# Attention and MLP on one core: five other token blocks, weights rounded through DRAM, and k halves stacked by transfers

## The chip, the cores and the metric

The kernel runs on one core of one Trainium2 chip, as one program. The metric is device time in microseconds (us). Of the kernel before there are three timed runs: 794.15, 796.12 and 800.07 us, median 796.12. A core has five engines that work side by side, each through its own list of instructions in order: PE (TensorE, matmuls; its weight loads are shown apart as PEld), DVE (VectorE), ACT (ScalarE), POOL (GpSimd) and SP (SyncE, which here issues every transfer). They wait for one another by semaphores.

## The reference, cut to what matters

```python
q, k, v: (4, 8, 576, 64)                       # batch, heads, tokens, head size
q_rot, k_rot = rotate(q), rotate(k)            # x1*cos - x2*sin, x1*sin + x2*cos
scores = q_rot @ k_rot.T / sqrt(64)
attn = softmax(scores)                         # max taken off, exp, divided by the sum
x = attn @ v, heads side by side               # (4, 576, 512): 2304 tokens of 512
xn = (x - mean(x)) / sqrt(var(x) + 1e-6) * g_ln
out = x + relu(xn @ w_ch1) @ w_ch2             # w_ch1: 512 x 2048, w_ch2: 2048 x 512
```

Everything is float32. A large matmul is made of three rounded ones (`fp32r`): an operand is split into a rounded part ("high") and the rest ("low"), and high by high, low by high and high by low are added up.

## The kernel before, in words

**Attention** goes through 16 pairs of heads, four for each of the four batches; two heads of 64 fill the 128 partitions. For pair `i`, `prepare` loads q and k with their swapped halves, rotates them (L315 to L319), rounds them (L322, L324), takes the low part (L327, L329) and lays high and low parts one above the other in the "stacks" that the score matmuls read (L423). For q, and for the k of pairs 4 to 15, SP does the stacking by transfers from SBUF to SBUF (L378 to L391). For the k of pairs 1 to 3 PE does it: two small matmuls with a doubled identity for each half and part (L357, 24 in all), each followed by a copy out of PSUM by ACT or DVE (L180). A pair then has nine score units: scores on PE (L423; the ninth L428 and L431), their maximum on DVE (L454), the exponential on ACT (L466). The results `p` are transposed on PE (L510, L524, L551) into PSUM tiles `t`, of which there are two, copied out by ACT or DVE (L180), and multiplied with `v` (L592, L596) in two parts, 256 and 320 queries, again into a `t` tile. DVE scales that by the inverse sums into the output tile `xt` (L607).

**The MLP** runs over blocks of tokens. `BLOCKS` has five: one of 256 tokens and four of 512. When all pairs of a block's tokens are in `xt`, `layer_norm` centres, scales and rounds it, with sums over the 512 features made by PE (L643, L677, L689). Then the block passes over the weights: 32 units of 12 matmuls (L814), each unit one 512x128 piece of a weight matrix in high and low parts; the moving side is the block, so a matmul has as many columns as the block has tokens. Units of the first matrix end in relu on ACT (L830) and the low part on DVE (L834); those of the second are added to `xt` (L844), and after the last four the block is stored (L853) and its `xt` tile is free. There is one `xt` buffer of 256 tokens and three of 512.

**The weights** come in as float64 (`w64`, 512 KB for a unit). `decode` makes float32 of them with two ACT operations (L742, L745), two on DVE (L748, L754) and one on POOL (L751), writes the result to DRAM (`keep`, L757) and at once splits it (`split`: high part by ACT, L774; low part by POOL or DVE, L778) for the first pass. The four later passes load the float32 piece from DRAM (`load_w`, L787) and split it again. A float32 piece sits in a ring of three buffers `f`, its high and low parts in a ring of three buffers `w`; in the first pass an `f` buffer is free only when both the write to DRAM and the split are done.

**The order of the work** is fixed when the program is built. Every step is a task with a duration for each engine that may do it, a priority and the ring buffers that it takes and gives. `Plan.run` walks through the tasks in planned time, starts whatever can start in order of priority, and so writes one list of instructions for each engine; attention's tasks have the priority of a nominal time (`nominal`, set by `FIRST`, `FAST`, `PACE`), the decode tasks one set by `DECODE0` and `DECODE1`, and the MLP matmuls the last of all, so that they fill what attention leaves. What a task really takes does not change the order: an engine that is at an instruction whose operand isn't there waits, with all that is behind it.

Of the kernel before, what the change touches and what calls it, by code (L numbers as in the profile page):

```python
# [10 lines left out]
F32 = mybir.dt.float32  # L11
# [23 lines left out]

BLOCKS = [(0, 256)] + [(t, BLOCK) for t in range(256, N_TOK, BLOCK)]
PARTS = slice(0, 2 * P), slice(2 * P, S)
# [101 lines left out]
def rope_attention_then_ln_mlp(  # L139
# [24 lines left out]

    cp, xp, qkp, vpool, xtp = pool("const"), pool("x", RINGS["x"]), pool("qk", RINGS["stk"]), pool("v", RINGS["v"]), pool("xt")
    pp, ptp, smp, lnp = pool("p", RINGS["p"]), pool("pt"), pool("small", 4), pool("ln")
# [6 lines left out]
    def raw(t):  # L173
        return t.bitcast(F32)
# [55 lines left out]
    def first_pair():  # L230
# [12 lines left out]
        def dma(kb, o, i, after=(), prio=-90.0):  # L243
            return add({"SP": kb / 230}, lambda: SP.dma_start(o, i), after, prio)

# [47 lines left out]
    def prepare(i):  # L293
# [5 lines left out]
        for n, nm in ((1, "k"), (0, "q")):  # L299
# [12 lines left out]
            def op(step, nm=nm):  # L312
                a, b = st["x", i, nm]
                if step == 0:
                    eng().tensor_tensor(out=a, in0=a, in1=rope_sb[:, 0], op=ALU.mult)  # L315
                elif step == 1:
                    eng().tensor_tensor(out=b, in0=b, in1=rope_sb[:, 1], op=ALU.mult)
                elif step == 2:
                    eng().tensor_tensor(out=a, in0=a, in1=b, op=ALU.add)  # L319
                elif step == 3 and nm == "k" and i < NPB:  # L320
                    h = st["hik", i] = lnp.tile([P, NC, BLOCK], F32R, name="xh").rearrange("p a s -> p (a s)")[:, :S]
                    ACT.copy(h, a)  # L322
                elif step == 3:
                    ACT.copy(b.bitcast(F32R), a)  # L324
                elif nm == "k":
                    kl = st["kl", i] = qkp.tile([P, S], F32R, name="k_lo")
                    eng().tensor_tensor(out=kl, in0=a, in1=raw(st["hik", i]) if i < NPB else b, op=ALU.subtract)  # L327
# [5 lines left out]
            ld = add({"SP": 576 / 230}, load, [ev.get("l_qs")] + free0, p - 8, take=ring, name=f"load{i}{nm}")  # L333
            r0 = add(how2, lambda op=op: op(0), [ld], p, name=f"r0.{i}{nm}")
# [12 lines left out]
            stacks = []  # L347
            if nm == "k" and i < NPB:

                done[nm, 0], done[nm, 1] = [], []  # L350
                for j in range(2):
                    for low in range(2):
                        for a in range(2):
                            def put(j=j, low=low, a=a):
                                ps = st["st", i, j, low, a] = mp.tile([P, 512], F32, name="m")
                                x = st["kl" if low else "hik", i]
                                PE.matmul(ps[:, :HS], lhsT=twice[j], rhs=x[:, KEYS[a]], start=True, stop=True)  # L357

                            def out(j=j, low=low, a=a):
                                t = ("skl", "sk")[1 - low]  # L360
                                if (t, i) not in st:
                                    st[t, i] = qkp.tile([P, 2, S], F32R, name=("stack_k", "stack_kl")[low])
                                copy(st[t, i][:, j, KEYS[a]], st.pop(("st", i, j, low, a))[:, :HS])

                            end = j == 1 and a == 1 and low == 1
                            m_ = add({"PE": 0.14}, put, [lo if low else hi, ev["c3"]], p + 0.6 + j, take=["m"], give=["x" + nm] if end and ring else [], lag=0.2, name=f"st{i}{j}{low}{a}")
                            o_ = add({"ACT": 0.40, "DVE": 0.44}, out, [m_], p + 0.6 + j, give=["m"], behind=done[nm, 1][:1])
                            done[nm, j].append(o_)
                            if j == 0:
                                done[nm, 1].append(o_)  # L370
                continue
            for j in range(2):
# [20 lines left out]
                kb = 288 if nm == "k" else 144  # L393
                stacks.append(add({"SP": kb / 200}, stack_hi, [hi], p + 0.6 + j, name=f"sh{i}{nm}{j}"))
                last = add({"SP": kb / 200}, stack_lo, [lo], p + 0.7 + j, behind=list(stacks), name=f"sl{i}{nm}{j}", give=ring if j else [])
                stacks.append(last)
# [3 lines left out]
    def load_v(i):  # L400
# [3 lines left out]

        ev["v", i] = add({"SP": 320 / 230}, load, [ev["l_qs"]], nominal(i, 0) - 4, take=["v"], name=f"v{i}")

# [26 lines left out]
    def attention(i):  # L433
# [45 lines left out]
        def sums(a):  # L479
# [5 lines left out]
            units = range(4) if a == 0 else range(4, 9)  # L485
            return add({"DVE": 0.36}, f, [exps[n] for n in units], nominal(i, units[-1]) + 0.5)

# [84 lines left out]
        for a in range(2):  # L572
# [25 lines left out]
            def scale(a=a):  # L598
                s = PARTS[a]
                ps = st.pop(("pv", i, a))  # L600
                for n, lo, hi in pieces(b, a):
                    if ("xt", n) not in st:
                        w = BLOCKS[n][1]
                        st["xt", n] = xtp.tile([P, NC, w], F32, name=f"xt{w}", bufs=RINGS[f"xt{w}"])
                    x = slice(lo - b * S - s.start, hi - b * S - s.start)
# [15 lines left out]
    def layer_norm(n):  # L621
        t0, W = BLOCKS[n]
        Q = W // 4
        parts = [(b, a) for b in range(B) for a in range(2) if any(m == n for m, _, _ in pieces(b, a))]
        done = [ev["x", NPB * b + c, a] for b, a in parts for c in range(NC)]
        b1, a1 = parts[-1]
        N = nominal(NPB * b1 + NPB - 1, 8 if a1 else 4) + 6
        z = {}
        two = {"POOL": 1.4 * W / 512, "DVE": 0.9 * W / 512}
        f = W / 512  # L630
# [5 lines left out]

        prev = done
# [63 lines left out]
        for c in range(NC):  # L701
# [12 lines left out]

            s = add({"DVE": 0.9 * f}, scale, [t], N + 0.1 * c)
            h = add({"ACT": 0.6 * f}, high, [s] + ([ready[0]] if c else []), N + 0.1 * c, take=["xn"] if c == 0 else [], name=f"xn{n}")
# [6 lines left out]
    def decode(k):  # L723
# [34 lines left out]

        t0 = add({"SP": 512 / 230}, load, [ev["l_qs"]] if k == 0 else [], prio - 8, behind=[ev["w64", k - 1]] if k else [], take=["w64"], name=f"w64.{k}")
        ev["w64", k] = t0  # L760
        t1 = add({"ACT": 0.67}, a1, [t0], prio, behind=[ev["a1", k - 1]] if k else [], take=["f"])
        ev["a1", k] = t1
        t2 = add({"ACT": 0.67}, a2, [t1], prio)
        t3 = add({"DVE": 0.56}, d1, [t1], prio)
        t4 = add({"POOL": 1.4}, p1, [t2, t3], prio)
        t5 = add({"DVE": 1.0}, d2, [t4], prio, give=["w64"])
        ev["ws", k] = add({"SP": 256 / 230}, keep, [t5], prio + 6)
        split(k, t5, prio)
        add({"NONE": 0.0}, lambda: None, [ev["ws", k]] + ev["wr", k], prio, give=["f"])

    def split(k, there, prio):
# [8 lines left out]
        ev["w", k] = add({"ACT": 0.62}, hi, [there], prio, behind=[ev["w", k - 1]] if k else [], take=["w"], name=f"w{k}")  # L780
        how = {"POOL": 1.35, "DVE": 0.9} if k < len(UNITS) else {"POOL": 1.35}
        ev["wr", k] = [add(how, lo, [ev["w", k]], prio, give=["f"] if k >= len(UNITS) else [])]

    def load_w(k, prio):
# [3 lines left out]

        ev["f", k] = add({"SP": 256 / 230}, load, [ev["ws", k % len(UNITS)]], prio, behind=[ev["f", k - 1] if k > len(UNITS) else ev["w", k - 1]], take=["f"], name=f"f{k}")
        split(k, ev["f", k], prio)  # L790


    def mlp_unit(k, prev):
# [45 lines left out]
        else:  # L839
# [7 lines left out]
            if u >= NF + 3 * NC:  # L847
# [7 lines left out]

                add({"SP": 256 / 230}, store, [r], 1e5, give=[f"xt{W}"] if c == NC - 1 else [], name=f"store{n}.{c}")

# [32 lines left out]

DEBUG = 1

# [51 lines left out]
```

## Time and profile before

| | us |
|---|---|
| median of three runs | 796.12 |
| the profiled execution, its own time | 797.25 |
| its span, first to last instruction | 795.5 |
| PE busy | 711.6 |
| DVE, POOL, ACT busy | 453.3, 444.8, 407.2 |
| mean granted TensorE clock | 0.972 |

A matmul counts as busy from its start to the modelled end of its drain, and matmuls that follow each other overlap; so how fast PE works through a row of them is read from their starts, not from their mean duration. In the line `L814 PE MATMUL m<-hh,w 128*128 128x512 f32 x512` the name `m` is a PSUM tile, `w` the weights, `hh` the moving side. Columns of a table of windows are: the stretch, its length, busy us and number of instructions of PE, PEld, DVE, ACT and POOL, the granted clock, the busy share of the DMA engines, and what they moved.

### The profile page before, as it was taken

Reading aid. Unit: us, or ns where it says so; the run is one execution under the profiler, and the core shown is the slowest. Engines: PE = TensorE matmul, PEld = TensorE weight load, DVE = VectorE, ACT = ScalarE, POOL = GpSimd, SP = SyncE. Lnnn points to the kernel's source line nnn. Section 1 sums busy time; section 2 is a strip of 40 time slices with the busy share of each in tenths; the row PEclk is TensorE's granted clock in tenths of the full one; section 3 lists DMA queues with packets and bytes.
Section 4 is the critical chain, followed back from the end, with each engine's and each line's share of the span. In section 5 each row is a group of like instructions: output and inputs, shape, how many; then the busy total and the mean of one; then the engine's idle time right before and its main releaser. Section 6 shows DMA issues by size and latency. Waiting matters only on the chain. (4 is left out here: it accounts for less than half of the span.)

```text
span 795.5 us, 11683 instructions
## 1 busy us (share of the span) xinstructions
PE 711.6 (89%) x3986; PEld 558.3 (70%) x3986; DVE 453.3 (57%) x756; ACT 407.2 (51%) x890; POOL 444.8 (56%) x326
## 2 busy tenths in 40 slices
PE   2788887998797877789989999999999999999998
PEld 1666555786575665668768888776787788878886
DVE  7768767778788897754783234644526522322222
ACT  3667657767575667545653344554424333433231
POOL 2587366777749665666874453114447444454442
PEclk9989999999899998899999999999999999999999
DMA  7655866668875676866636334112234232353332
GB/s 216 205 160 160 267 160 167 170 208 243 238 218 143 196 232 200 214 181 194 155 114 185 98 101 126 54 54 69 79 94 133 85 101 93 93 149 103 92 95 78
DMA packets 65691, 117.83 MB, mean 148 GB/s; under 512 B 11472, under 2 KB 23520, under 8 KB 65632
## 3 DMA queue, kind: packets, MB, share of 16 engines
q1 hardware_dynamic: 65632, 117.09, 51.1%
q8 instruction: 31, 0.51, 0.3%
q14 instruction: 28, 0.23, 0.1%
HBM read 79.76 MB, written 13.18 MB: 117 GB/s over the span
## 5 line engine op out<-in xcount | busy, mean ns | idle before, releaser
L778 POOL TENSOR_TENSOR w<-f,w 128x512 fp32r<-128x512 f32 x145 | 190.8, 1318 | 230.1 <-ACT w L774 213.0
L814 PE MATMUL m<-hh,w 128*128 128x512 f32 (+1 forms) x640 | 197.7, 380 | 6.0 <-DVE w L778 3.2
L774 ACT CAST w<-f 128x512 fp32r<-128x512 f32 x160 | 99.0, 620 | 200.2 <-PE m L814 101.1
L814 PE MATMUL m<-xh,w 128*128 128x512 f32 (+1 forms) x640 | 195.2, 375 | 1.9 <-ACT std L681 1.1
L814 PEld LDWEIGHTS m<-hh,w 128*128 128x128 f32 x640 | 119.4, 192 | 29.8 <-DVE w L778 4.0
L814 PEld LDWEIGHTS m<-xh,w 128*128 128x128 f32 x640 | 118.4, 189 | 24.3 <-ACT std L681 1.4
L454 DVE TENSOR_REDUCE mx<-sc 128x1 f32<-128x576 f32 x144 | 105.7, 748 | 38.7 <-PE sc L423 31.6
L466 ACT ACTIVATE p<-sc,mx 128x576 f32<-128x576 f32 x144 | 106.0, 739 | 35.0 <-DVE mx L454 22.9
L814 PE MATMUL m<-hl,w 128*128 128x512 f32 (+1 forms) x320 | 119.3, 373 | 1.8 <-DVE hl L834 1.8
L814 PE MATMUL m<-xl,w 128*128 128x512 f32 (+1 forms) x320 | 118.3, 370 | 0.0
L834 DVE SCALAR_TENSOR_TENSOR hl<-m,hh 128x512 fp32r<-128x512 f32 (+1 forms) x80 | 50.8, 635 | 110.4 <-ACT hh L830 110.2
L510 PE MATMUL t<-ident,p 128*128 128x128 f32 x512 | 84.4, 292 | 28.1 <-DVE xt L607 7.1
L844 DVE TENSOR_TENSOR xt<-xt,m 128x512 f32<-128x512 f32 (+1 forms) x80 | 50.5, 631 | 94.7 <-PE m L814 94.6
L510 PEld LDWEIGHTS t<-ident,p 128*128 128x128 f32 x512 | 61.5, 147 | 47.0 <-issue 9.3
L180 ACT COPY pt<-t 128x512 f32<-128x512 f32 (+1 forms) x86 | 47.1, 550 | 65.4 <-PE t L510 56.4
L423 PE MATMUL sc<-stack_k,stack_q 128*128 128x288 f32 x252 | 64.6, 339 | 8.2 <-ACT p L466 7.9
L596 PE MATMUL t<-pt,v 128*64 128x320 f32 (+1 forms) x512 | 71.6, 424 | 0.0
L814 PEld LDWEIGHTS m<-hl,w 128*128 128x128 f32 x320 | 61.5, 192 | 13.0 <-DVE hl L834 2.6
L180 DVE COPY pt<-t 128x512 f32<-128x512 f32 (+1 forms) x74 | 46.0, 621 | 37.6 <-PE t L510 31.4
L814 PEld LDWEIGHTS m<-xl,w 128*128 128x128 f32 x320 | 60.7, 190 | 9.2
L751 POOL TENSOR_TENSOR f<-f,w 128x512 int32<-128x512 int32 x32 | 42.9, 1339 | 37.6 <-ACT w L745 19.3
L596 PEld LDWEIGHTS t<-pt,v 128*64 128x64 f32 x512 | 35.1, 141 | 33.3 <-issue 15.1
(128 smaller groups left out, 972.5 us busy)
## 6 DMA issues: line engine op xcount, KB each, us to landing
f<-w SPq DMA_DIRECT2D x128, 256.0 KB
w<-in_w1p SPq DMA_DIRECT2D x16, 512.0 KB
w<-f SPq DMA_DIRECT2D x32, 256.0 KB
w<-in_w2p SPq DMA_DIRECT2D x16, 512.0 KB
xk<-in_qk SPq DMA_DIRECT2D x14, 576.0 KB
xq<-in_qk SPq DMA_DIRECT2D x14, 576.0 KB
stack_q<-xq SPq DMA_DIRECT2D x56, 144.0 KB
stack_kl<-k_lo SPq DMA_DIRECT2D x52, 144.0 KB
```

What stands on the lines that cost most here:

```text
L180: (ACT.copy if plan.engine == "ACT" else DVE.tensor_copy)(o, i)
L423: PE.matmul(ps[:, a, :HS], lhsT=sq[:, j, q], rhs=y[:, j, KEYS[a]], start=y is sk, stop=y is skl)
L454: DVE.tensor_reduce(out=mx, in_=st["ps", i, n][:, :, :HS], axis=AX.XY, op=ALU.max, negate=True)
L466: ACT.activation(out=halves(p), in_=st.pop(("ps", i, n))[:, :, :HS], func=AF.Exp, bias=st.pop(("mx", i, n)), scale=1.0, accum_out=total)
L510: PE.transpose(ps[:, k], p[:, j, j * T + k * P : j * T + (k + 1) * P], ident)
L596: PE.matmul(ps[r], lhsT=v[:, k, r], rhs=pt[:, j, k], start=False, stop=k == 3)
L751: POOL.tensor_tensor(out=z["f"], in0=z["f"], in1=z["c"], op=ALU.add)
L774: ACT.copy(w[:, 0].rearrange("p a n -> p (a n)"), st["f", k].bitcast(F32))
L778: eng().tensor_tensor(out=w[:, 1], in0=st.pop(("f", k)).bitcast(F32), in1=raw(w[:, 0]), op=ALU.subtract)
L814: PE.matmul(ps, lhsT=wt, rhs=x, start=c + m == 0, stop=c + m == NC + 1)
L834: DVE.scalar_tensor_tensor(out=h2, in0=z["ps"][:, :W], scalar=0.0, in1=raw(h1), op0=ALU.max, op1=ALU.subtract)
L844: DVE.tensor_tensor(out=o, in0=o, in1=z["ps"][:, :W], op=ALU.add)
```

## The change

The diff does five things.

- `BLOCKS` becomes 512, 512, 512, 384 and 384 tokens. All `xt` tiles now have room for 512 tokens, in one ring of three.
- A decoded weight piece goes into a buffer of its own (`d`, ring of two) and from there to DRAM, and nothing else; it is not split from there. All five passes, the first too, load from DRAM. `f` keeps three buffers, `w` gets four. `load_w` gets a priority ahead of attention's (-2.0).
- k of pairs 1 to 3 is stacked by SP transfers as that of the others (`KPE` is 0).
- Layer norm may start its sums feature block by feature block, and its priority is 10 us earlier.
- The ring `p` has three buffers instead of four. The planner's durations and its transfer rate have other values, and decode has other priorities.

```diff
-BLOCKS = [(0, 256)] + [(t, BLOCK) for t in range(256, N_TOK, BLOCK)]
+BLOCKS = [(0, 512), (512, 512), (1024, 512), (1536, 384), (1920, 384)]
...
-RINGS = {"sc": 2, "t": 2, "m": 2, "p": 4, "p9": 1, "pt0": 1, "pt1": 1, "x": 1, "stk": 2, "v": 2, "inv": 2, "w64": 2, "f": 3, "w": 3, "h": 4, "xn": 1, "ln": 1, "xt256": 1, "xt512": 3}
+RINGS = {"sc": 2, "t": 2, "m": 2, "p": 3, "p9": 1, "pt0": 1, "pt1": 1, "x": 1, "stk": 2, "v": 2, "inv": 2, "w64": 2, "f": 3, "d": 2, "w": 4, "h": 4, "xn": 1, "ln": 1, "xt": 3}
-DECODE0, DECODE1 = 30.0, 4.5
+DECODE0, DECODE1 = 70.0, 4.0
+RATE = 300.0
+KPE = 0
+EARLY = 10.0
...
-                elif step == 3 and nm == "k" and i < NPB:
+                elif step == 3 and nm == "k" and i < KPE:
...
-            if nm == "k" and i < NPB:
+            if nm == "k" and i < KPE:
...
-            ev["x", i, a] = add({"DVE": 0.5}, scale, [t, rd], N, behind=lead, take=[f"xt{BLOCKS[n][1]}" for n in fresh], give=["t"] + (["inv"] if a else []))
+            ev["x", i, a] = add({"DVE": 0.5}, scale, [t, rd], N, behind=lead, take=["xt"] * len(fresh), give=["t"] + (["inv"] if a else []))
...
-        done = [ev["x", NPB * b + c, a] for b, a in parts for c in range(NC)]
+        done = [[ev["x", NPB * b + c, a] for b, a in parts] for c in range(NC)]
...
+        N = min(N - EARLY, 1e5)
+        prev = done[0]
         for c in range(1, NC):
-            prev = [add(two, lambda c=c: acc(c), prev, N, take=["ln"] if c == 1 else [], name=f"ln{n}")]
+            prev = [add(two, lambda c=c: acc(c), prev + done[c], N, take=["ln"] if c == 1 else [], name=f"ln{n}")]
...
-            f = z["f"] = st["f", k] = wp.tile([P, NC * P], I32, name="f", bufs=RINGS["f"])
+            f = z["f"] = wp.tile([P, NC * P], I32, name="d", bufs=RINGS["d"])
...
-        t5 = add({"DVE": 1.0}, d2, [t4], prio, give=["w64"])
-        ev["ws", k] = add({"SP": 256 / 230}, keep, [t5], prio + 6)
-        split(k, t5, prio)
-        add({"NONE": 0.0}, lambda: None, [ev["ws", k]] + ev["wr", k], prio, give=["f"])
+        t5 = add({"DVE": 1.25}, d2, [t4], prio, give=["w64"])
+        ev["ws", k] = add({"SP": 256 / RATE}, keep, [t5], prio, give=["d"])
...
-        how = {"POOL": 1.35, "DVE": 0.9} if k < len(UNITS) else {"POOL": 1.35}
-        ev["wr", k] = [add(how, lo, [ev["w", k]], prio, give=["f"] if k >= len(UNITS) else [])]
+        how = {"POOL": 1.35, "DVE": 1.0} if k < 2 * len(UNITS) else {"POOL": 1.35}
+        ev["wr", k] = [add(how, lo, [ev["w", k]], prio, give=["f"])]
...
     for k in range(len(UNITS) * NB):
-        if k >= len(UNITS):
-            load_w(k, 9e5 + k)
+        load_w(k, -2.0)
         mlp_unit(k, None)
```

Three places show what this does to the lists. The numbers behind the names are buffer numbers; line numbers of the changed kernel are two or three higher than before.

The first is PE's list around the first `pt`-by-`v` product of pair 6 (tiles `pt0`), in the midst of attention. Before:

```order
L592 MATMUL t_2315<-p40_2169,v_1765 128x256
L596 MATMUL t_2315<-pt0_2168,v_1765 64x256 x8
L423 MATMUL sc_2332<-stack_k_1842,stack_q_2016 128x288 x2
L423 MATMUL sc_2332<-stack_kl_1876,stack_q_2016 128x288 x2
L510 MATMUL t_2339<-ident_165,p_2070 128x128 x4
L423 MATMUL sc_2348<-stack_k_1842,stack_q_2016 128x288 x2
L423 MATMUL sc_2348<-stack_kl_1876,stack_q_2016 128x288 x2
L814 MATMUL m_2303<-xh_1607,w_2283 128x256
L814 MATMUL m_2303<-xl_1608,w_2283 128x256
L814 MATMUL m_2303<-xh_1607,w_2283 128x256 x2
```

And now:

```order
L595 MATMUL t_2096<-p40_1983,v_1692 128x256
L599 MATMUL t_2096<-pt0_1982,v_1692 64x256 x8
L513 MATMUL t_2113<-ident_165,p_2010 128x128 x4
L426 MATMUL sc_2122<-stack_k_1469,stack_q_1499 128x288 x2
L426 MATMUL sc_2122<-stack_kl_1520,stack_q_1499 128x288 x2
L431 MATMUL sc_2131<-k_lo_1485,diag0_170 128x288 x2
L434 MATMUL sc_2131<-stack_k_1469,last_q0_172 128x288 x4
L513 MATMUL t_2143<-ident_165,p_2010 128x128 x4
L815 MATMUL m_2076<-xh_1775,w_1067 128x512
L815 MATMUL m_2076<-xl_1776,w_1067 128x512
L815 MATMUL m_2076<-xh_1775,w_1067 128x512 x2
```

The MLP matmuls of the first pass stand among attention's as before, but each has 512 columns instead of 256. Counted over the whole list, 918 MLP matmuls stand ahead of attention's last one before (384 of 256 columns, 534 of 512) and 1002 behind it; now 924 stand ahead, all of 512 columns, and 996 behind it (228 of 512 columns, 768 of 384). The first MLP matmul stands in pair 5 before and in pair 6 now.

The second is SP's list from the write of pair 7's first sums on. Before:

```order
L574 DMA sums7_0_113<-row0_2669 4x128
L378 DMA stack_q_2671<-xq_2519 64x576
L735 DMA w64_2692<-in_w1p 128x1024
L757 DMA w8_147<-f_2635 128x512
L385 DMA stack_q_2671<-xq_2519 64x576 x2
L310 DMA xk_2765<-in_qk 128x1152
L584 DMA inv_2784<-sums7_0_113 64x2x128 x2
```

And now:

```order
L577 DMA sums7_0_113<-row0_2464 4x128
L788 DMA f_2498<-w23_146 128x512
L587 DMA inv_2531<-sums7_0_113 64x2x128 x2
L760 DMA w10_149<-d_2446 128x512
L738 DMA w64_2539<-in_w2p 128x1024
L760 DMA w11_150<-d_2515 128x512
L738 DMA w64_2591<-in_w2p 128x1024
L788 DMA f_2594<-w8_147 128x512
L381 DMA stack_k_2607<-xk_2312 64x576
```

Loads of `f` (L788) now stand between attention's transfers; each may go only when a split has freed an `f` buffer. Ahead of the write of pair 12's first sums there are 11 such loads before and 48 now. The transfers that stand from pair 6's first write of sums to that of pair 10 hold 28.6 MB before and 37.9 MB now, and the loads of the k stacks of pairs 1 to 3 are 24 more transfers of 144 KB near the list's start.

The third is DVE's list now, where the first pass ends; `xt_592` is the tile of the first 512 tokens, `xt_3851` that of tokens 1536 to 1919, in the same buffer ring:

```order
L845 TENSOR_TENSOR xt_592<-xt_592,m_3773 128x512
L845 TENSOR_TENSOR xt_592<-xt_592,m_3788 128x512
L779 TENSOR_TENSOR w_3835<-f_3753,w_3835 128x512
L835 SCALAR_TENSOR_TENSOR hl_3838<-m_3808,hh_3837 128x512
L609 TENSOR_TENSOR xt_1726<-t_3234,inv_3017 128x128
L609 TENSOR_TENSOR xt_3851<-t_3234,inv_3017 128x192
L609 TENSOR_TENSOR xt_1726<-t_3737,inv_3421 128x128
L609 TENSOR_TENSOR xt_3851<-t_3737,inv_3421 128x192
```

Pair 8's second part (`t_3234`) is the first to write `xt_3851`, and waits until the first block has gone through its whole pass and is stored; its PSUM tile `t` is held till then, and pair 9's (`t_3737`) with it. Before, with one more `xt` buffer, no such wait stood in pairs 8 to 11; one for the last block stood, and stands, in pair 12. Of the 160 low parts of weights DVE makes 15 before and 34 now, POOL the others.

More of the change, by code (lines that the diff above doesn't have):

```diff
@@ L243, in dma @@
         def dma(kb, o, i, after=(), prio=-90.0):
-            return add({"SP": kb / 230}, lambda: SP.dma_start(o, i), after, prio)
+            return add({"SP": kb / RATE}, lambda: SP.dma_start(o, i), after, prio)
         def tt(o, a, b, op, after, dur=0.76, prio=-80.0, e="DVE"):
@@ L326, in op @@
                     kl = st["kl", i] = qkp.tile([P, S], F32R, name="k_lo")
-                    eng().tensor_tensor(out=kl, in0=a, in1=raw(st["hik", i]) if i < NPB else b, op=ALU.subtract)
+                    eng().tensor_tensor(out=kl, in0=a, in1=raw(st["hik", i]) if i < KPE else b, op=ALU.subtract)
                 else:
@@ L332, in prepare @@
             free0 = ev["stk", 0][1] + ev["diag", 0] + [ev["s", 0, 1]] if i == 2 else []
-            ld = add({"SP": 576 / 230}, load, [ev.get("l_qs")] + free0, p - 8, take=ring, name=f"load{i}{nm}")
+            ld = add({"SP": 576 / RATE}, load, [ev.get("l_qs")] + free0, p - 8, take=ring, name=f"load{i}{nm}")
             r0 = add(how2, lambda op=op: op(0), [ld], p, name=f"r0.{i}{nm}")
@@ L393, in prepare @@
                 kb = 288 if nm == "k" else 144
-                stacks.append(add({"SP": kb / 200}, stack_hi, [hi], p + 0.6 + j, name=f"sh{i}{nm}{j}"))
-                last = add({"SP": kb / 200}, stack_lo, [lo], p + 0.7 + j, behind=list(stacks), name=f"sl{i}{nm}{j}", give=ring if j else [])
+                stacks.append(add({"SP": kb / RATE}, stack_hi, [hi], p + 0.6 + j, name=f"sh{i}{nm}{j}"))
+                last = add({"SP": kb / RATE}, stack_lo, [lo], p + 0.7 + j, behind=list(stacks), name=f"sl{i}{nm}{j}", give=ring if j else [])
                 stacks.append(last)
@@ L403, in load @@
             SP.dma_start(v, vp[divmod(i, NPB)])
-        ev["v", i] = add({"SP": 320 / 230}, load, [ev["l_qs"]], nominal(i, 0) - 4, take=["v"], name=f"v{i}")
+        ev["v", i] = add({"SP": 320 / RATE}, load, [ev["l_qs"]], nominal(i, 0) - 4, take=["v"], name=f"v{i}")
     def pieces(b, a):
@@ L485, in sums @@
             units = range(4) if a == 0 else range(4, 9)
-            return add({"DVE": 0.36}, f, [exps[n] for n in units], nominal(i, units[-1]) + 0.5)
+            return add({"DVE": 0.6}, f, [exps[n] for n in units], nominal(i, units[-1]) + 0.5)
         inverse = [sums(0), sums(1)]
@@ L602, in scale @@
                     if ("xt", n) not in st:
-                        w = BLOCKS[n][1]
-                        st["xt", n] = xtp.tile([P, NC, w], F32, name=f"xt{w}", bufs=RINGS[f"xt{w}"])
+                        st["xt", n] = xtp.tile([P, NC, BLOCK], F32, name="xt")
                     x = slice(lo - b * S - s.start, hi - b * S - s.start)
@@ L628, in layer_norm @@
         z = {}
-        two = {"POOL": 1.4 * W / 512, "DVE": 0.9 * W / 512}
+        two = {"POOL": 1.5 * W / 512, "DVE": 1.05 * W / 512}
         f = W / 512
@@ L713, in low @@
                 eng().tensor_tensor(out=st["xl", n][:, c], in0=z["xc"][:, c], in1=raw(st["xh", n][:, c]), op=ALU.subtract)
-            s = add({"DVE": 0.9 * f}, scale, [t], N + 0.1 * c)
+            s = add({"DVE": 1.1 * f}, scale, [t], N + 0.1 * c)
             h = add({"ACT": 0.6 * f}, high, [s] + ([ready[0]] if c else []), N + 0.1 * c, take=["xn"] if c == 0 else [], name=f"xn{n}")
@@ L757, in keep @@
             SP.dma_start(scratch[u], z["f"].bitcast(F32))
-        t0 = add({"SP": 512 / 230}, load, [ev["l_qs"]] if k == 0 else [], prio - 8, behind=[ev["w64", k - 1]] if k else [], take=["w64"], name=f"w64.{k}")
+        t0 = add({"SP": 512 / RATE}, load, [ev["l_qs"]] if k == 0 else [], prio - 8, behind=[ev["w64", k - 1]] if k else [], take=["w64"], name=f"w64.{k}")
         ev["w64", k] = t0
-        t1 = add({"ACT": 0.67}, a1, [t0], prio, behind=[ev["a1", k - 1]] if k else [], take=["f"])
+        t1 = add({"ACT": 0.67}, a1, [t0], prio, behind=[ev["a1", k - 1]] if k else [], take=["d"])
         ev["a1", k] = t1
         t2 = add({"ACT": 0.67}, a2, [t1], prio)
-        t3 = add({"DVE": 0.56}, d1, [t1], prio)
+        t3 = add({"DVE": 0.7}, d1, [t1], prio)
         t4 = add({"POOL": 1.4}, p1, [t2, t3], prio)
-        t5 = add({"DVE": 1.0}, d2, [t4], prio, give=["w64"])
-        ev["ws", k] = add({"SP": 256 / 230}, keep, [t5], prio + 6)
-        split(k, t5, prio)
-        add({"NONE": 0.0}, lambda: None, [ev["ws", k]] + ev["wr", k], prio, give=["f"])
+        t5 = add({"DVE": 1.25}, d2, [t4], prio, give=["w64"])
+        ev["ws", k] = add({"SP": 256 / RATE}, keep, [t5], prio, give=["d"])
     def split(k, there, prio):
@@ L787, in load @@
             SP.dma_start(f.bitcast(F32), scratch[UNITS[k % len(UNITS)]])
-        ev["f", k] = add({"SP": 256 / 230}, load, [ev["ws", k % len(UNITS)]], prio, behind=[ev["f", k - 1] if k > len(UNITS) else ev["w", k - 1]], take=["f"], name=f"f{k}")
+        ev["f", k] = add({"SP": 256 / RATE}, load, [ev["ws", k % len(UNITS)]], prio, behind=[ev["f", k - 1]] if k else [], take=["f"], name=f"f{k}")
         split(k, ev["f", k], prio)
@@ L888, in rope_attention_then_ln_mlp @@
         print([r for r in rows_ if r[0][0] in "emx" or r[0].startswith("ln")][:: 20])
-DEBUG = 1
+DEBUG = 0
 _OUT = (B, NC, P, S)
```

5 lines of the change are left out of this document (2 added, 3 removed).

## The prediction

> **What bounds the kernel now.** First the page: how busy each engine is, and where in the span PE, its clock and the DMA engines stand.
>
> ```profile
> PE 711.6 (89%) x3986; PEld 558.3 (70%) x3986; DVE 453.3 (57%) x756; ACT 407.2 (51%) x890; POOL 444.8 (56%) x326
> ...
> PE   2788887998797877789989999999999999999998
> ...
> DMA  7655866668875676866636334112234232353332
> ```
>
> PE is near full in the second half and has gaps in the first, where the DMA engines are busiest. Next, windows cut at the first MLP matmul (141 us), at pair 13's last scores (416), and at attention's last matmul (554.6); then the same windows for the MLP matmuls (L814) alone, with their numbers.
>
> ```profile
> 0.00:141.00 141.00, 104.06 (x660) 76.91 (x661) 102.83 (x205) 90.22 (x220) 79.81 (x64) 0.96 0.68 192
> 141.00:416.00 275.00, 235.50 (x1540) 182.32 (x1540) 211.19 (x336) 174.16 (x398) 194.01 (x133) 0.94 0.67 194
> 416.00:554.60 138.60, 138.46 (x755) 109.63 (x754) 58.03 (x107) 61.68 (x131) 54.90 (x42) 1.00 0.34 98
> 554.60:795.50 240.90, 233.63 (x1038) 189.42 (x1036) 81.22 (x109) 81.18 (x141) 116.05 (x88) 1.00 0.34 99
> ```
>
> ```profile
> 0.00:141.00 141.00, 1.68 (x9) 1.56 (x10) 0.96 0.68 192
> 141.00:416.00 275.00, 91.98 (x497) 72.95 (x496) 0.94 0.67 194
> ...
> 554.60:795.50 240.90, 230.62 (x1002) 186.87 (x1002) 1.00 0.34 99
> ```
>
> From 416 us on PE is the bound. From 141 to 416 us no engine is: PE idles 275 - 235.5 = 39.5 us, DVE 64, and PE's longest waits are many short ones:
>
> ```profile
> PE sc L423 <- ACT p L466: 7.9, 14, 1.1
> ...
> PE t L510 <- DVE xt L607: 7.1, 4, 5.2
> ...
> PE m L814 <- DVE w L778: 3.9, 5, 1.9
> ```
>
> So the last stretch is as long as the MLP work left over for it, and the question is what more fits into the first 554.6 us.
>
> **The price of a matmul.** The chain of waits ends in a long row of 512-column matmuls, then DVE's last addition; the timeline at 183 us shows 256-column ones.
>
> ```profile
> 709.42 82.10 PE m L814 x360
> ...
> 791.54 0.69 DVE xt L844
> ```
>
> ```profile
> 183.46 0.28 PE L814 MATMUL m<-xl,w 128*128 128x256 f32 x1
> 183.58 0.40 PE L814 MATMUL m<-xh,w 128*128 128x256 f32 x2
> 183.81 0.28 PE L814 MATMUL m<-xl,w 128*128 128x256 f32 x1
> 183.93 0.28 PE L814 MATMUL m<-xh,w 128*128 128x256 f32 x1
> 184.05 0.43 PE L423 MATMUL sc<-stack_k,stack_q 128*128 128x288 f32 x2
> ```
>
> 512 columns: 82.10 / 360 = 0.228 us. 256 columns: five starts from 183.46 to 184.05, 0.118 us. For 384, which no row shows, I take the middle, 0.173 (it can't well be below 0.118 or above 0.228; three quarters of 0.228 would be 0.171).
>
> **Blocks.** All five passes: before 384 x 0.118 + 1536 x 0.228 = 395.5 us, now 1152 x 0.228 + 768 x 0.173 = 395.5 us. The new widths by themselves save nothing. What changes is where the work stands. Behind attention's last matmul stood 1002 x 0.228 = 228.5 us; by PE's new list 228 x 0.228 + 768 x 0.173 = 184.9 us stand there. That is 43.6 us less at the end, and 43.6 us more ahead of it (924 x 0.228 = 210.7 against 384 x 0.118 + 534 x 0.228 = 167.1). The gain is what of these 43.6 us goes into idle PE time.
>
> Room: 39.5 us by busy time between 141 and 416. Besides, the 497 MLP matmuls there (375 of the 384 narrow ones, 9 lying earlier) count 92 us busy, but by their starts are 375 x 0.118 + 122 x 0.228 = 72 us; the other 20 are drains of short groups, in which a further matmul can start. 60 us of room for 43.6: I let all of it fit. The ends are 0 and 43.6 us not fitting.
>
> **Weights through DRAM.** The split no longer follows decode directly; PE's waits for `w` on DVE (3.9 us above) can go. Pass 0 gains 32 loads of 256 KB. In the last passes a unit lasts 12 x 0.173 = 2.08 us instead of 2.74; against that stands its split:
>
> ```profile
> L778 POOL TENSOR_TENSOR w<-f,w 128x512 fp32r<-128x512 f32 x145 | 190.8, 1318 | 230.1 <-ACT w L774 213.0
> ...
> L774 ACT CAST w<-f 128x512 fp32r<-128x512 f32 x160 | 99.0, 620 | 200.2 <-PE m L814 101.1
> ```
>
> 0.62 + 1.32 = 1.94 us even one after the other, and ACT mostly waits for PE to free a `w` buffer, not the reverse. I cost it at nothing; PE's own matmuls hide it.
>
> 19 more splits go to DVE:
>
> ```profile
> L778 DVE TENSOR_TENSOR w<-f,w 128x512 fp32r<-128x512 f32 x15 | 15.5, 1031 | 1.6 <-ACT w L774 1.5
> ```
>
> ```profile
> L778 DVE TENSOR_TENSOR w<-f,w x15: 653/947/1879, 39.3 to 327.4; 128x512 fp32r<-128x512 f32 x15
> ```
>
> 19 x 1.03 = 20 us of DVE into the 64 us it idles, with POOL freed of 19 x 1.32 = 25 us: nothing on the path. The spread of the second row, 0.65 to 1.88 us for one form, shows that it is often held up, and the mean has that in it. The Trainium skill, "SBUF — State Buffer", section "Who interferes with whom", says that a DVE operation with two SBUF inputs and a GpSimd one reading SBUF take turns at a shared port, one blocked for the other's whole length. That speaks against this edit and agrees with the spread; by it, if each of the 19 held POOL for its 1.03 us, POOL would lose 20 of the 25 us it is spared, and the sum would stay.
>
> **k stacks by transfers.** It removes 24 matmuls and 24 copies, and adds 24 transfers of 144 KB.
>
> ```profile
> L357 PE MATMUL m<-xh,twice 128*128 128x288 f32 x12 | 4.7, 460 | 3.1 <-ACT xh L322 2.9 <-ACT stack_kl L180 0.2
> ...
> L357 PE MATMUL m<-k_lo,twice 128*128 128x288 f32 x12 | 4.2, 391 | 0.0
> ```
>
> PE's part is 4.7 + 4.2 + 3.1 = 12 us, the most that it can bring. The 3.5 MB take 13 us at the fastest rate of a window (269 GB/s, below), beside others; late stacks could cost as much. From -12 to +13 I take -5, since PE idles 37 of the first 141 us, so that part of what is removed was no loss.
>
> **Rings.** One `p` buffer less: ACT's waits for PE to empty one were
>
> ```profile
> ACT p L466 <- PE t L524: 11.1, 8, 4.5
> ```
>
> They may as much as double, 0 to +11 us; taken +2, as ACT idles 101 of the 275 us. The wait for `xt` in pairs 8 to 10 holds both `t` tiles, and behind pair 8's product in PE's list the transposes of over a pair have one or none. A transpose tile costs its copy,
>
> ```profile
> L180 DVE COPY pt<-t 128x512 f32<-128x512 f32 x56 | 38.4, 687 | 31.7 <-PE t L510 31.4
> ```
>
> 0.69 us; a pair has eight such (56 here and 72 on ACT, over 16 pairs) and some smaller: for two pairs 0 to 14 us. The MLP matmuls that end the wait stand in the same list, so PE has work; I take +3. Layer norm's earlier start isn't on the path at 141 us, where MLP matmuls now begin a pair later: nothing either way, 2 us at most.
>
> **The sum** goes against the profiled span, 795.5 us: -43.6 - 5 + 2 + 3 = -43.6, so 751.9 us. That execution took 797.25 us, 1.75 beyond its span; the median of the three runs, 796.12, is 0.6 above the span. So 752 us.
>
> **Rivals.** For them some windows, and SP's waits.
>
> ```profile
> 141.00:285.00 144.00, 121.01 (x840) 94.72 (x840) 117.15 (x184) 95.76 (x221) 103.60 (x70) 0.94 0.71 205
> 80.00:100.00 20.00, 16.88 (x113) 11.30 (x112) 13.92 (x29) 13.39 (x33) 6.82 (x6) 1.00 0.89 269
> ...
> 300.00:320.00 20.00, 14.47 (x80) 10.78 (x80) 15.11 (x24) 12.43 (x27) 12.40 (x9) 0.79 0.73 213
> 160.00:180.00 20.00, 20.00 (x154) 16.63 (x151) 14.54 (x24) 13.07 (x32) 14.06 (x10) 0.96 0.73 228
> ```
>
> ```profile
> SPq L787 <- POOL w L778: 247.0, 109, 5.6
> SPq L735 <- DVE f L754: 42.0, 23, 6.1
> ```
>
> *Transfers bind in pairs 6 to 9.* Their 28.6 MB become 37.9; the pairs filled roughly the 144 us from 141 to 285. At 269 GB/s 37.9 MB need 141 us, at the 205 that moved there 185. For: only one window comes near the fast rate. Against: the DMA share there was 0.71, so it had slack. Halfway the price is 20 us: 772, 763 to 787.
>
> *Nothing fits.* Pair by pair, DVE, ACT and transfers take turns, so each matmul put between lengthens the pair: all 43.6 us come back, 795.5, no change. For: 39.5 us of idle lie in pieces of about 1 us, less than a group of six (1.37 us). Against: 160 to 180 us has PE busy for all 20 us while attention went on.
>
> *SP is held up: slower.* 37 more loads of `f` stand ahead of pair 12 and each waits on SP until POOL or DVE has freed a buffer; behind it wait stacks, q, k and sums, and for those PE. L787's waits are 247 / 109 = 2.27 us. 37 of these, all on the path, are 84 us: 752 + 84 = 836. It decides from 43.6 / 37 = 1.2 us a load on. For: SP waits so already for decode (1.8 us each, L735). Against: those 247 us lie where SP runs ahead of a full PE; attention's transfers are mostly issued well ahead.
>
> *A fuller PE gets a better clock.* Where PE had gaps it was granted less: 0.79 at 14.5 busy of 20 us, 0.96 at 20, and 1.00 throughout behind 416. From 141 to 416 the mean was 0.94; at 1.00 the 235.5 busy us would be 14 shorter: 738. The Trainium skill, "TensorE: Matmul & The Clock Gate", section "Part 1: The HAM clock gate", has it that idle windows of some microseconds halve the clock and activity restores it; the rows agree. Against: one loses by a slow matmul only where PE is last.
>
> **Chances.** The forecast (742 to 763) 0.42; transfers (763 to 787) 0.20; better clock (728 to 742) 0.16; nothing fits (788 to 804) 0.10; SP (above 804) 0.10; 0.02 for below 728. That the weights aren't ahead is worth under 6 us and lies within the forecast. Range 733 to 785: both last rivals, 0.20, stay out. About 1%, 788 to 804, is what a measurement of this kernel can't tell from no change. Faster: 0.42 + 0.20 + 0.16 + 0.02 = 0.80; same 0.10; slower 0.10.
>
> **What would show it.** In the profile after: attention's last matmul at about 555 us with 996 MLP matmuls behind it, 184.9 us of PE work plus some 12 for the rest; 384-column matmuls 0.173 us apart; PE busy above 0.9 between its first MLP matmul and pair 13, with a clock above 0.94. Wrong if attention ends near 600 us; if there PE waits for ACT and DVE, nothing fits; if a DMA share near 0.9 goes with late stacks, transfers; if SP waits over 1.2 us on L788 with attention's transfers behind, SP.

## The result and the profile after

The changed kernel takes 764.4 us (median of 4 runs, 763.19 to 766.28) against 797.7 us for the kernel before in the same comparison: a ratio of 0.959, 95% interval 0.954 to 0.963. The prediction said 752, range 733 to 785, faster with 0.80. The direction, the size to about a quarter (33 us gained, 44 forecast) and the range held. The profiled execution has a span of 763.0 us against 795.5; what follows is told against these two spans. One run of e6 (812.85 us, granted clock 0.839) and one of e8 (764.39 us, 0.971), both told of below, were in a slower state, and their ratios go by the other three.

The page after, its first parts:

```profile
PE 693.4 (91%) x3962; PEld 561.1 (74%) x3962; DVE 453.9 (59%) x721; ACT 415.6 (54%) x916; POOL 434.1 (57%) x315
...
PE   2878767779989989999999999999999999999997
...
DMA  8987977766979975855566333452123353445442
```

The first nine slices of PE, taken together, are emptier than before; from the tenth on PE is nearly full, where before it had gaps until past the eighteenth. The DMA engines are busier in the first six slices. Now the windows after, cut at the first MLP matmul (167 us), at pair 12's last scores (402) and at attention's last matmul (563.4):

```profile
0.00:167.00 167.00, 116.89 (x723) 83.75 (x724) 117.81 (x198) 108.34 (x258) 110.41 (x81) 0.92 0.81 227
167.00:402.00 235.00, 224.63 (x1313) 174.71 (x1313) 179.80 (x271) 150.84 (x343) 148.28 (x100) 0.98 0.74 219
402.00:563.40 161.40, 159.89 (x901) 124.94 (x899) 87.50 (x148) 83.39 (x181) 64.86 (x50) 1.00 0.39 107
563.40:763.00 199.60, 191.97 (x1030) 177.65 (x1030) 68.84 (x107) 73.03 (x137) 110.60 (x85) 1.00 0.40 116
```

The kernel before, cut at the same points of its own work:

```profile
0.00:137.00 137.00, 100.52 (x644) 73.74 (x645) 100.53 (x200) 87.36 (x212) 78.91 (x64) 0.98 0.67 190
137.00:380.00 243.00, 205.44 (x1350) 161.11 (x1349) 185.82 (x306) 153.53 (x355) 166.08 (x116) 0.92 0.70 202
380.00:554.60 174.60, 172.06 (x963) 134.01 (x961) 85.72 (x143) 85.19 (x184) 83.73 (x61) 1.00 0.38 108
```

In the second stretch PE is now busy for 224.6 of 235 us (0.96) instead of 205.4 of 243 (0.85), with a clock of 0.98 instead of 0.92. Behind attention stand 199.6 us instead of 240.9. Attention itself ends later, at 563.4 us instead of 554.6. The last product with `v`, from the timeline after:

```profile
561.01 2.37 PE L599 MATMUL t<-pt,v 128*64 128x320 f32 x16
```

So 41.3 us are gained behind attention and 8.8 us lost ahead of it: 32.5 us of span. The prediction had 43.6 and 0. The MLP matmuls behind attention, and one stretch of 384-column ones on the timeline:

```profile
563.40:763.00 199.60, 189.14 (x996) 175.11 (x996) 1.00 0.40 116
```

```profile
702.12 0.51 PE L815 MATMUL m<-hh,w 128*128 128x384 f32 x2
702.46 0.33 PE L815 MATMUL m<-hl,w 128*128 128x384 f32 x1
702.63 0.51 PE L815 MATMUL m<-hh,w 128*128 128x384 f32 x2
702.98 0.33 PE L815 MATMUL m<-hl,w 128*128 128x384 f32 x1
```

996 matmuls are there, as the list had it, and three 384-column ones take 702.98 - 702.46 = 0.52 us, 0.173 each. That price was right. PE's waits after, the longest but the one at the very start:

```profile
PE t L513 <- ACT p L469: 10.4, 5, 4.3
...
PE sc L426 <- ACT p L469: 8.4, 11, 1.4
PE t L513 <- DVE p L183: 4.9, 4, 2.4
```

No wait of a matmul of the MLP for its weights is left among them; what remains are waits for the exponential and for copies.

### The profile page after: what moved, and what is told of

Its sections match the earlier page's. It is cut to its first block, busy times and chain, and to the rows that moved or that the text cites. A ratio compares the mean times of both kernels' runs of the same rounds, so it can differ in the third digit from the quotient of the medians.

```text
span 763.0 us, 11765 instructions
## 1 busy us (share of the span) xinstructions
PE 693.4 (91%) x3962; PEld 561.1 (74%) x3962; DVE 453.9 (59%) x721; ACT 415.6 (54%) x916; POOL 434.1 (57%) x315
## 5 line engine op out<-in xcount | busy, mean ns | idle before, releaser
L779 POOL TENSOR_TENSOR w<-f,w 128x512 fp32r<-128x512 f32 x126 | 166.3, 1321 | 176.2 <-ACT w L775 165.3
L815 PE MATMUL m<-xh,w 128*128 128x512 f32 (+1 forms) x640 | 198.6, 377 | 4.4 <-DVE hl L835 3.3
L815 PEld LDWEIGHTS m<-xh,w 128*128 128x128 f32 x640 | 120.0, 190 | 20.3 <-DVE hl L835 4.1
L469 ACT ACTIVATE p<-sc,mx 128x576 f32<-128x576 f32 x144 | 106.3, 740 | 32.0 <-DVE mx L457 28.6
L183 ACT COPY pt<-t 128x512 f32<-128x512 f32 (+1 forms) x101 | 54.7, 543 | 50.5 <-PE t L513 42.5
L754 POOL TENSOR_TENSOR d<-d,w 128x512 int32<-128x512 int32 x32 | 45.3, 1416 | 46.2 <-ACT w L748 18.6
L599 PE MATMUL t<-pt,v 128*64 128x320 f32 (+1 forms) x512 | 70.3, 417 | 0.0
L599 PEld LDWEIGHTS t<-pt,v 128*64 128x64 f32 x512 | 34.5, 139 | 32.8 <-issue 14.2
L426 PE MATMUL sc<-stack_kl,stack_q 128*128 128x288 f32 x252 | 55.8, 304 | 0.0
```

Of the source, the lines that this page charges most:

```text
L183: (ACT.copy if plan.engine == "ACT" else DVE.tensor_copy)(o, i)
L426: PE.matmul(ps[:, a, :HS], lhsT=sq[:, j, q], rhs=y[:, j, KEYS[a]], start=y is sk, stop=y is skl)
L469: ACT.activation(out=halves(p), in_=st.pop(("ps", i, n))[:, :, :HS], func=AF.Exp, bias=st.pop(("mx", i, n)), scale=1.0, accum_out=total)
L599: PE.matmul(ps[r], lhsT=v[:, k, r], rhs=pt[:, j, k], start=False, stop=k == 3)
L754: POOL.tensor_tensor(out=z["f"], in0=z["f"], in1=z["c"], op=ALU.add)
L779: eng().tensor_tensor(out=w[:, 1], in0=st.pop(("f", k)).bitcast(F32), in1=raw(w[:, 0]), op=ALU.subtract)
```

## The experiments

Theory 1 is the prediction's: the gain is MLP work that stood behind attention and now fills PE's idle time in it, by way of the wide first block. Theory 2 is that it comes from the weights, which no longer tie the first pass to decode. And three things had to be told apart for the 8.8 us by which attention ends later: PE work that did not fit, transfers, and the work of decode on the other engines. Kernels named e are planned anew, so their lists differ in many places; kernels named x keep the list of the kernel they are made from, word for word but for what is left out or doubled. Attention's ends are those of the last L599 (or L596) matmul, as above. Each x kernel ran once; the four runs of the changed kernel lie 3 us apart, so a microsecond or two of an x kernel says little.

**e1_blocks_only.** The kernel before with

```diff
-BLOCKS = [(0, 256)] + [(t, BLOCK) for t in range(256, N_TOK, BLOCK)]
+BLOCKS = [(0, 512), (512, 512), (1024, 512), (1536, 384), (1920, 384)]
```

and the one ring of three output tiles that goes with it.

> The kernel before with the new blocks alone (512, 512, 512, 384, 384 tokens, one ring of three output tiles); weights decoded and split as before, k of pairs 1 to 3 stacked on PE, four p buffers, the old planner's numbers. Its PE list has 918 MLP matmuls of 512 columns ahead of attention's last matmul and 186 us of MLP work behind it, as the changed kernel (185 us). Theory 1 (the gain is MLP work moved from behind attention into PE's idle time): most of the gain is here, 763 to 775 us. Theory 2 (the gain comes from the weights, which no longer bind the first pass to decode): the first pass still hangs on decode, all moved work lengthens attention, 790 to 800 us.

775.1 us, ratio 0.972 (0.968 to 0.976). Span 772.8. Attention's last product starts at

```profile
569.91 2.37 PE L596 MATMUL t<-pt,v 128*64 128x320 f32 x16
```

and ends at 572.3; 200.5 us stand behind it. So the blocks alone bring nearly all of the gain behind attention (240.9 to 200.5) and pay 17.7 us ahead of it. Ahead of it lies a single wait of PE of 8.5 us, at the end of the first block's pass, for the first weight piece of the second:

```profile
354.75 0.80 PE L813 MATMUL m<-xh,w 128*128 128x512 f32 x1 [8.53 <-ACT w L773]
```

Its load stands behind attention's transfers on SP and goes out at 350.4 us only. The changed kernel, whose loads have a priority ahead of attention's, has no such wait.

**e2_old_blocks.** The changed kernel with the first line of that diff reversed.

> The changed kernel with the old blocks (256 tokens and four times 512); weights through DRAM, k stacks by transfers, rings and planner's numbers as in the changed kernel. Its PE list has 168 us of MLP work ahead of attention's last matmul and 227 us behind it, as the kernel before. Theory 1 (moved work): the gain is gone, 785 to 800 us. Theory 2 (weights): the gain stays, 760 to 772 us.

811.9 us, ratio 1.016 (1.011 to 1.021): longer than before, and clear of 1, though by less than 2%. 237.6 us stand behind attention, as theory 1 wants, but attention ends at 573.7 us. Neither theory had that. PE's longest waits there:

```profile
PE m L815 <- ACT w L775: 10.3, 3, 5.6
PE m L815 <- DVE w L779: 10.0, 7, 4.2
```

PE waits 20 us for weights in the first pass, against 5.6 us in the kernel before (3.9, 0.9 and 0.8 for DVE, POOL and ACT).

**e7_old_blocks_early.** To see why, e2 with decode's priorities of before.

```diff
-DECODE0, DECODE1 = 70.0, 4.0
+DECODE0, DECODE1 = 30.0, 4.5
```

> The changed kernel with the old blocks and also the decode priorities of before. With the old blocks alone it took 812 us, 14 more than the kernel before, with PE's waits for weights (w) at 20 us against 6, since a 256-token pass uses a unit up in 1.4 us. If decode standing later is what starves that pass: the waits go and the time comes back to about that of before, 790 to 802 us. If the way through DRAM itself is slow: 806 to 815 still.

791.7 us (8 runs), ratio 0.992 (0.989 to 0.994). PE's waits for weights are down to

```profile
PE m L815 <- DVE w L779: 3.2, 2, 1.6
```

and 0.4 us for POOL. The slowness of e2 was the later decode, not the way through DRAM: a pass of 256 columns uses a unit up in 1.4 us, and decode at the later priorities could not keep up with it. With them set back, everything but the blocks and those priorities is worth 0.8%, inside the 1% taken here as no change. The blocks are worth 2.8% alone (e1), 2.4% between e7 and e6 below, which differ in them only, and 5.6% between e2 and the changed kernel. So theory 2 falls as the main cause and theory 1 stands, with one restriction: with the wide blocks the weights do count, as e1's wait shows.

**x3_pass0_twice.** Does idle time in attention take more PE work? In the list of before, each matmul of the 256-token pass is made twice.

```diff
-                    PE.matmul(ps, lhsT=wt, rhs=x, start=c + m == 0, stop=c + m == NC + 1)
+                    for again in range(2 if n == 0 else 1):
+                        PE.matmul(ps, lhsT=wt, rhs=x, start=c + m + again == 0, stop=c + m == NC + 1 and (n > 0 or again == 1))
```

> The kernel before, its order untouched, with each of the 384 matmuls of the 256-token pass made twice (the result is no longer the reference's): 384 x 0.118 = 45 us more PE work ahead of attention's last matmul, and nothing else. If PE's idle time there takes nearly all of it, as theory 1 has it: attention's last matmul at 555 to 568 us, span 796 to 809. If each matmul put between lengthens the pair: attention ends near 600 us, span near 840.

Span 825.4 us; attention ends at 585.0, 30.4 us later: between the two expectations. Only 15 of the 45 us were taken by idle time. In the list of before, most of PE's idle time was not free for more work in the same places.

**x4_pass0_half.** The reverse, in the list of the changed kernel: the first pass makes 6 of a unit's 12 matmuls.

```diff
-                    PE.matmul(ps, lhsT=wt, rhs=x, start=c + m == 0, stop=c + m == NC + 1)
+                    if n > 0 or m == 0 or (m == 2 and c % 2 == 1):
+                        PE.matmul(ps, lhsT=wt, rhs=x, start=c + m == 0, stop=c + m == NC + 1)
```

> The changed kernel, its order untouched, with the first pass leaving out 6 of each unit's 12 matmuls (three of four of the low parts' terms; the result is no longer the reference's): 192 x 0.228 = 44 us less PE work ahead of attention's last matmul, nothing else. The changed kernel's attention ended 8.8 us later than before (563.4 against 554.6). If that is the part of the moved work that did not fit: attention ends near 553 us, span 751 to 757. If something else made it late (transfers, the decode work on ACT, DVE and POOL, the other stacks): 560 to 564, span 759 to 763.

Span 759.5 us; attention's last product:

```profile
558.95 2.37 PE L599 MATMUL t<-pt,v 128*64 128x320 f32 x16
```

Taking 44 us of PE work out of attention moves its end by 2 us, from 563.4 to 561.3. In the new list the moved work does fit: 42 of 44 us are hidden. But the emptier PE was granted a lower clock:

```profile
167.00:402.00 235.00, 199.00 (x1144) 147.07 (x1143) 182.26 (x276) 150.88 (x349) 150.03 (x102) 0.94 0.75 220
```

That is 0.94 where the changed kernel has 0.98. 4% of these 235 us are some 9 us, an estimate of the most that slower matmuls can have taken back; by it at least 33 us are hidden. That the 8.8 us are not PE's is likely and not shown.

**x1_no_w64_loads, x2_no_decode, x5_no_f_loads.** Three kernels in the changed kernel's list, each leaving out one thing that attention has beside it.

```diff
+            if k < 2:
+                st["w64", k] = cp.tile([P, NC, 2 * P], U32, name=f"w64_{k}")
...
+            z["x"] = st["w64", k % 2]
```

> The changed kernel, its order untouched, with the float64 weights of two units alone loaded and all 32 units decoded from those two (the result is no longer the reference's): 30 x 512 KB fewer transfers in attention, the same work on ACT, DVE and POOL. Halving the first pass's PE work has moved attention's end by 2 us only, so PE isn't what sets it. If the transfers set it (228 GB/s ahead of the first MLP matmul, 216 after it): attention ends at 535 to 550 us, span 735 to 750. If the engines' work does: 558 to 564, span 757 to 763.

```diff
         def a1():
+            return
...
-            SP.dma_start(f.bitcast(F32), scratch[UNITS[k % len(UNITS)]])
+            SP.dma_start(f.bitcast(F32), qk[0, 0, :, 0, : NC * P])
```

(with the same `return` in decode's other steps)

> The changed kernel, its order untouched, with decode left out altogether: no float64 loads, no decode operations on ACT, DVE and POOL, no writes to DRAM; all weight pieces are loaded from a part of q instead, in the same size and number (the result is no longer the reference's). If decode's engine work (32 x (0.67 + 0.67) us on ACT, 32 x (0.71 + 1.33) on DVE, 32 x 1.42 on POOL) sets attention's end: 520 to 540 us, and x1 stays near 560. If transfers: about as x1, 535 to 550. If neither, 558 to 564.

```diff
+            if k < 48:
...
+                st["f", k] = st["f_kept", 0]
+                return
```

> The changed kernel, its order untouched, without the first 48 loads of float32 weight pieces from DRAM (those ahead of pair 12), which are split from one piece instead (the result is no longer the reference's): SP no longer waits for a buffer before each, and the first pass no longer waits for the way through DRAM; 12 MB fewer. If SP held up by these loads sets attention's end, as the rival of the prediction had it: 535 to 550 us. If not: 558 to 564, with the span 4 us below that of the changed kernel at most.

Each one's last product of attention, in this order:

```profile
549.18 2.37 PE L599 MATMUL t<-pt,v 128*64 128x320 f32 x16
```

```profile
537.23 2.37 PE L599 MATMUL t<-pt,v 128*64 128x320 f32 x16
```

```profile
559.79 2.46 PE L599 MATMUL t<-pt,v 128*64 128x320 f32 x16
```

Attention ends at 551.6, 539.6 and 562.3 us; the spans are 749.0, 737.4 and 761.5. In this list the float64 loads alone cost attention 11.8 us, all of decode 23.8, so its engine work, its writes to DRAM and what waits for them the other half; the `f` loads, against which the prediction had set its slower rival, cost 1 us, no more than two runs differ by. x1 ends 1.6 us above the range that was expected for transfers. The kernel before makes the same float64 loads, so the 11.8 us are what they cost and not what the change added. (x5's profile has a granted clock of 0.95 wherever the changed kernel's has 1.00, but three of its 384-column matmuls take 0.52 us too, from 702.04 to 702.56, so PE was no slower.) x1's window from 125 to 305 us, with the changed kernel's above it, shows that more of the engines' work gets done in the time without these loads:

```profile
125.00:305.00 180.00, 160.32 (x941) 121.57 (x942) 147.49 (x208) 126.17 (x279) 127.38 (x84) 0.95 0.78 229
```

```profile
125.00:305.00 180.00, 165.63 (x990) 126.61 (x988) 153.49 (x217) 132.55 (x294) 131.36 (x87) 0.97 0.60 174
```

The transfers there go from 229 to 174 GB/s and the DMA share from 0.78 to 0.60; PE, DVE, ACT and POOL each do some 3 to 5% more.

**e3_k_on_pe.** The changed kernel with

```diff
-KPE = 0
+KPE = 4
```

> The changed kernel with the k of pairs 1 to 3 stacked by PE and copies again (planned anew, all else the same). The prediction put the change to transfers at a gain of 5 us, bounds -13 to +12: 768 us here. In the profile after, pair 1's last scores came 9 us earlier than before and pair 3's 3 us later; if the stacks' transfers were what made pairs 2 and 3 late, this kernel loses 9 us at pair 1 and has it back at pair 3: 761 to 766.

769.4 us, ratio 0.965 (0.963 to 0.967) where the changed kernel had 0.959. The stacks by transfers seem worth some 5 us in the end, as predicted, though that is no more than a newly planned list may bring by itself (e4, below); and the profiled executions, 764.0 and 763.0 us of span, are only 1 us apart. Pair 5's last scores, in the changed kernel and here:

```profile
156.31 0.52 PE L431 MATMUL sc<-k_lo,diag 128*128 128x288 f32 x2
```

```profile
147.84 0.51 PE L431 MATMUL sc<-k_lo,diag 128*128 128x288 f32 x2
```

In the first pairs the stacks by transfers cost 8.5 us, and x1, without the float64 loads, has the same scores at 149.4. Before, they came at 147.3. So the lateness arises ahead of the first MLP matmul, and taking away either the stacks' transfers or the float64 loads removes most of it. Yet e3 loses the lead again by pair 6 (190.1 against 191.3), and ends attention at 565.5.

**e4_f4.** `"f": 4` instead of 3 in the changed kernel.

> The changed kernel with four f buffers instead of three (planned anew). In the changed kernel's profile ACT waits twice, 4 us together, for an f load near 690 us, where a full f ring kept SP from issuing it early, and PE then waits for the weights. If that wait is worth its length: 3 to 5 us less, 759 to 762. Leaving out the first 48 loads moved attention's end by 1 us, so no more than that is expected ahead of it. If the wait comes from the layer norm's work on POOL in front of the splits and not from the ring: no change, 763 to 766.

771.4 us, ratio 0.967 (0.961 to 0.972), some 7 us slower than the changed kernel and outside both expectations. ACT's waits for `f` near 690 us are gone and 197.9 us stand behind attention instead of 199.6, but attention ends at 571.8. One buffer more was enough to let the planner write another list, and that list is 8 us worse ahead of attention's end, for reasons that were not followed up. It sets the scale for what a single e kernel can tell: some 8 us may be the luck of the list.

**e6_early_decode.** The changed kernel with e7's edit.

> The changed kernel with the decode priorities of before (first 30, step 4.5, instead of 70 and 4), planned anew. Leaving out all of decode brought attention's end from 563 to 540 us, leaving out its float64 loads alone to 552. If what decode costs is its sum of work and transfers, wherever they stand: 760 to 770 us. If it costs by falling into the first pairs, where the transfers are at their densest: more of it there costs more, 770 to 785.

Ratio 0.967 (0.960 to 0.975), three runs from 765.3 to 775.6 us: on the average 772, just inside the second expectation, but within the 8 us just named. With wide blocks no more than that hangs on when decode runs.

**e8_f4_k23_on_pe.** Four `f` buffers, and k of pairs 2 and 3 on PE, of pair 1 by transfers.

```diff
-KPE = 0
+KPE = (2, 3)
...
-                elif step == 3 and nm == "k" and i < KPE:
+                elif step == 3 and nm == "k" and i in KPE:
```

> The changed kernel with four f buffers and the k of pairs 2 and 3 stacked by PE, that of pair 1 by transfers. With all k on PE pair 1 came 5 us later and pair 5 8 us earlier than in the changed kernel. If the two parts add up, and what pair 5 gains isn't lost again: 752 to 760 us. If later pairs wait for decode anyway, whose work stands where it stood: 760 to 768.

754.1 us, ratio 0.944 (0.940 to 0.948): better than the kernel before and the changed one. Pair 5's last scores and attention's last product:

```profile
146.16 0.50 PE L431 MATMUL sc<-k_lo,diag 128*128 128x288 f32 x2 [1.76 <-ACT p L469]
```

```profile
552.24 2.37 PE L599 MATMUL t<-pt,v 128*64 128x320 f32 x16
```

Attention ends at 554.6 us, as before the change, 198.1 us stand behind it, and the span is 752.7. What of the 10 us over the changed kernel is due to the two edits and what to another list was not separated.

## Why the prediction was right, and where it was off

**Blocks: right.** That the widths themselves save nothing (395.5 us of MLP matmuls either way), that 43.6 us move from behind attention to ahead of it, and 0.173 us for a 384-column matmul are all seen. Behind attention 41.3 us went; 2.3 us of the forecast were lost there, which goes with two waits of ACT for an `f` load between 680 and 700 us:

```profile
ACT w L775 <- DMA f<-w: 4.0, 2, 2.4
```

The prediction had costed the supply of the narrow passes at nothing, from the lengths of the split alone. With a fourth buffer 1.7 of the 2.3 us came back (e4: 197.9 us).

**Room: right by its result, not by its reason.** "60 us of room for 43.6: I let all of it fit." x4 shows 33 to 42 of 44 hidden in the new list. But x3 shows that idle time added up is no measure of it: in the old list, with that idle time, 30 of 45 us came out on top. It is the new order that makes the work fit.

**Attention's end: where it was off.** The terms ahead of it, -5 for the k stacks, +2 for `p` and +3 for `xt`, add up to nothing, and it came 8.8 us later. As waits, the profile after shows, the two ring terms were no cost; what smaller rings did to the order of the list was not tried. With one `p` buffer less, ACT's waits for PE to empty one fell from 11.1 us to

```profile
ACT p L469 <- PE t L527: 2.0, 3, 1.4
```

Pair 8's second product ended at 290.9 us and held its `t` tile until the first block was done, at 347.1, and from 335.7 us pair 9's product held the other:

```profile
333.36 2.37 PE L599 MATMUL t<-pt,v 128*64 128x320 f32 x16
347.14 1.01 DVE L609 TENSOR_TENSOR xt<-t,inv 128x128 f32<-128x128 f32 x4
290.90:347.10 56.20, 55.25 (x298) 43.80 (x299) 44.57 (x59) 31.15 (x71) 33.59 (x23) 1.00 0.66 199
```

PE was busy for 55.25 of these 56.2 us, since MLP matmuls stand there, as the prediction said.

The stacks by transfers were early at pair 1, as hoped: its last scores came at 48.8 us against 53.6 with all k on PE. But pair 5's came 8.5 us later than with k on PE, and 9.0 us later than before. These transfers meet decode's float64 loads: 227 GB/s and a DMA share of 0.81 up to the first MLP matmul, against 190 and 0.67 before. That lateness hangs on their sum, as e3 and x1 show, which each take away one part of it. It is the prediction's "late stacks", which it had as the bound only. At attention's end the stacks by transfers are worth 2 us by e3, where the prediction put 5, but two lists differ by more (e4).

Whether these 9 us are also the 8.8 us at attention's end is not shown, and the record speaks against it: e3 takes them away and ends attention at 565.5 us, and in e7 pair 5's last scores come 20 us later than before,

```profile
167.59 0.51 PE L431 MATMUL sc<-k_lo,diag 128*128 128x288 f32 x2
550.22 2.38 PE L599 MATMUL t<-pt,v 128*64 128x320 f32 x16
```

while attention ends at 552.6, 2 us earlier. Which step lost the 8.8 us stays open. Within the changed kernel's list less decode moves attention's end (x1, x2), and the `f` loads do not (x5). In e8 attention ends where the prediction had it, but that is one more list.

**The rivals.** "Transfers bind in pairs 6 to 9" had a price of 20 us for 9.3 MB more, of which 32 `f` loads of 256 KB are the most part; x5 leaves those out and wins 1 us, so this falls as it was put. Transfers do cost attention 11.8 us (x1), but by the float64 loads, which were there before; 6.9 us of it are there by pair 5's last scores (149.4 against 156.3), the rest comes by pair 9. "Nothing fits" was two thirds right for the old list (x3) and falls for the new one (x4). "SP is held up" falls with x5. "A fuller PE gets a better clock" is seen in the clock (0.98 for 0.92 between the first MLP matmul and pair 12). The 14 us beyond the forecast that it was to bring did not come; what it did bring is not shown, since x4 took away work and clock together. Nor is busy time all that goes with the clock: in the prediction's own rows 16.88 busy us of 20 had 1.00 and a full 20 had 0.96.

**Weights ahead: right that they are worth little by themselves** with the old blocks (e7, 0.8%). With the new blocks e1 and the changed kernel are 10.7 us apart, and PE's waits for weights in e1 are as long:

```profile
PE m L813 <- ACT w L773: 10.7, 2, 8.5
```

The prediction put the waits that can go at under 6 us, from the narrow first pass, and did not look for a wait at the end of the wide one. That later decode can also cost, where it stands too late for a narrow pass (e2, +14 us), it did not see.

## What to carry to other kernels

Count the work that stands behind the last step that everything waits for, and what the change takes away there; that part was forecast to 2 us. Whether moved work fits into idle time can't be read from the sum of the idle time: leave the work out, or double it, in the finished list, see what moves, and read the granted clock beside it. Moving a copy from the engines to transfers is judged by what else those transfers meet at that moment, and two sets of transfers can be late together, as pair 5's scores were. Being late in the first pairs does not yet mean being late at the end.

## What was not expected

A 256-token pass can be starved by a decode that the plan puts 40 us later (`DECODE0` 70 instead of 30) while a 512-token pass is not: with the same new way of the weights the one kernel was at 1.016 of before (1.011 to 1.021; e2) and the other at 0.959 (0.954 to 0.963), faster than the blocks alone at 0.972 (0.968 to 0.976; e1). And a planner's list is sensitive: one more buffer, which took a wait away, made the kernel 7 us slower (e4), and the same buffer with another placing of two pairs' copies made it 10 us faster (e8).
